# Gated linear attention with expert routing: the first expert search in a written order, all routing positions set anew, and a PSUM bank handed from the search results to the row transposes

## The chip, the cores and the metric

The kernel runs on one core of a Trainium2 chip. The metric is the device time of one execution in microseconds (us). The kernel before takes 435.39 us, the median of three runs (435.33 to 435.68). A difference of about 0.2% (0.9 us) is the least that such runs can tell from no change.

The engines are named as in the profile: PE is TensorE's matmul queue, PEld its weight loads, DVE is VectorE, ACT is ScalarE, POOL is GpSimd, SP is SyncE. Each of them works through its own instructions in order.

## The reference

The attention state is decayed by alpha and updated token by token. Its output is the input of a layer with eight experts, and routing goes by one sorted list of all (token, expert) logits:

```
for t in range(S):
    state = alpha[:, :, t, :, None] * state + einsum('bhd,bhe->bhde', k[:, :, t], v[:, :, t])
    y[:, :, t] = einsum('bhd,bhde->bhe', q[:, :, t], state)
x = y.transpose(0, 2, 1, 3).reshape(3072, 384)
logits = x @ w_gate                      # 3072 x 8
for idx in argsort(-logits.flatten()):
    tok, e = idx // 8, idx % 8
    if assigned[tok] < 0 and counts[e] < 384:
        assigned[tok] = e; counts[e] += 1
for e in range(8):
    mask = assigned == e
    out[mask] = maximum(x[mask] @ w1[e], 0) @ w2[e]     # 384 -> 1024 -> 384
```

Every expert ends with exactly 384 tokens, its capacity.

## The kernel before

**Routing in rounds.** The sorted list is not walked. A round takes for every token its best expert that is still open, finds the expert that fills up first and the logit at which it is full, and closes that expert. So there are eight rounds, one per expert, and the expert of a round is only known when its round is done. The key of a logit (a 32-bit integer) is cut into five digits (`BITS`, 7, 7, 6, 6, 6 bits). For each digit, one level of the search runs: DVE compares the digit with all its values (`compare`, the tile `cmp`), PE counts the tokens per expert at or above each value (24 matmuls into columns 32 to 39 of the tile `rt`, lines 581 and 614), DVE tests the counts against the places left (`g`), PE adds up the flags (`flags`, L599), DVE takes the largest (`k`, L601) and makes the next digit. After the last level the counts are kept (`cs`, L595), and `find` (L623) names the expert, starts its weight DMAs (`weights`, L528) and sums tokens per partition (`rts`). `offsets` (L655) is a matmul with a triangle of ones (`tri`), `places` numbers the tokens (`cum` ... `wb`, `bk`), `one_hot` (L694) builds the big table `hot` (128x3072) and `rhs`, `index` (L705) turns them into token numbers with 24 matmuls, and `gather` (L712) converts them on DVE (`idx`) and fetches the rows of x by three indirect DMAs on POOL's queue.

For the next round, `take_places` (L726) makes a one-hot column `oh` and closes the expert in the logits `L`; `gone` (L732) is one matmul that yields the tokens gone to each expert (columns 40 to 47 of `rt`); `best_left` (L737) is a chain of DVE operations from the maximum over `L` to the first digit `top`; `new_choice` (L759) makes `val`, `chu` and `o`; `left` (L774) subtracts what `gone` gave from `rem`.

**Where these results lie.** PSUM is used in banks of 128x512 FP32 values. One bank, `scr`, holds DVE's scratch columns (`slot`, L499). `rt` is a tile of its own in another bank, taken anew at every level. Further banks hold `h` (two), the three outputs `y0` to `y2`, and one bank, `xt`, in which rows and index results lie. Waits are set between instructions that touch the same PSUM bank, not only the same columns.

**The expert's work.** `split_hi` (ACT) and `split_lo` (POOL) cut the FP32 weights into a high and a low part, `whi` and `wlo`; `rows` (PE transposes, ACT copies) and `rows_lo` (DVE) do the same to the gathered rows (`xh`, `xl`). An expert has 144 products: eight units `ffn1` of nine matmuls (L835: three products of parts by three blocks of 128) and eight units `ffn2` of nine (L855). `ffn1`'s result goes through ACT (`hh`, L840) and DVE (`hl`, L841) to `ffn2`. A unit `ffn2` comes two `ffn1` units behind. From the third expert on, the first `ffn1` of an expert stands ahead of the last `ffn2` of the one before it.

**What sets the order.** All 1152 products stand in one list. Everything else that PE, DVE, ACT and POOL do during it is put in by position: `at(position, fn)` (L902) issues a routing step when that many products have been written. `levels` and `found` (L915, L919) place the five levels and the steps from `find` to `index` of the next expert; `renewed` (L926) places `take_places` and `gather` at an expert's base, `best_left` one product later and `gone` six products after the base. Of the engines' orders PE's is the one that carries the products, so a routing matmul whose input is late stops all products behind it.

**The start.** Attention ends at about 134 us. The first round's search can only then run its last four levels. Of the 96 transposes that bring the attention output back to rows (`y_trans`, L340, four to a group), 64 are left to be done between the search's steps. In this part the tile scheduler sets the order: `search(0)` (L563) ties each level's counts to a group of these transposes (`Y_IN_SEARCH`). Then follow, in written order, `find` to `gather` for expert 0, dummy matmuls (`spin_more`, L879), the first rows and the first level of the next round, and the products.

## Time and profile before

| quantity | before |
| --- | --- |
| median of 3 runs | 435.39 us (435.33 to 435.68) |
| the profiled execution | 433.69 us |
| its span | 431.8 us |
| mean granted TensorE clock | 0.969 |
| end of attention, first matmul of the first search's flags | 134.05 us |
| first product (ffn1 of expert 0) | 165.65 us |
| POOL busy | 279.9 us (65%) |
| ACT busy | 195.7 us (45%) |

The profile is of one execution. In the page, busy times are summed over instructions, and PE's ends are modelled: a matmul that overlaps the next is counted whole. In a timeline each row has the start, the busy time, the engine with line and operation, the output and the inputs, and in brackets how long the engine was idle before it and what released it. Rows of the same kind that follow each other are joined (x3), and their time is then that of the group. In a table of windows, each row is a stretch of the span with the busy time of each engine, and PEclk is the share of the full TensorE clock that was granted in it. The span lacks 1.9 us of the profiled execution's time, which lie before and behind it.

### The profile page before, as it was taken

What the parts mean: (1) busy time and instruction counts of PE and PEld (TensorE: products, weight loads), DVE (VectorE), ACT (ScalarE), POOL (GpSimd) and SP (SyncE); (2) the same over time, 40 slices, a digit from 0 to 9 for tenths busy, and PEclk for the clock granted to TensorE, in tenths of its full rate; (3) what the DMA queues carried; (4) which work ended last, traced back from release to release, by engine and by line L of the source; (5) the groups of instructions that cost most, each with busy time, mean ns of one, the idle gap of its engine ahead of it and who ended that gap; (6) DMA issues with size and microseconds to landing.
All of it is one profiled execution on the core that took longest, in us unless ns stands there. A gap on an engine that the chain in (4) does not pass through costs nothing.

```text
span 431.8 us, 10887 instructions
## 1 busy us (share of the span) xinstructions
PE 396.6 (92%) x4154; PEld 347.8 (81%) x4154; DVE 284.2 (66%) x838; ACT 195.7 (45%) x447; POOL 279.9 (65%) x327
## 2 busy tenths in 40 slices
PE   7999999989898858989999999999999997999993
PEld 3787777768676737989898899999999887999993
DVE  7888888878736497686697597687587576221210
ACT  1476666556565422424423534434434433644411
POOL 4668988677620026854687786776866865997802
PEclk9699999999999769999999999999999999999998
DMA  8999966660004584180180190191191198310101
GB/s 284 331 270 263 255 193 206 179 188 18 2 3 169 197 264 160 54 295 2 31 317 20 47 330 28 44 329 35 40 326 38 39 325 304 106 71 2 55 2 55
DMA packets 34467, 63.39 MB, mean 147 GB/s; under 512 B 3328, under 2 KB 14592, under 8 KB 34416
## 3 DMA queue, kind: packets, MB, share of 16 engines
q1 hardware_dynamic: 28176, 48.54, 36.0%
q0 software_dynamic: 3072, 9.44, 6.3%
q10 hardware_dynamic: 3168, 4.72, 3.1%
q8 instruction: 33, 0.54, 0.5%
q14 instruction: 18, 0.15, 0.1%
HBM read 53.25 MB, written 9.44 MB: 145 GB/s over the span
## 4 chain that ended last, share of the span: by engine, by line
PE 62%; DVE 21%; issue 6%; DMA 4%; POOL 3%; ACT 2%; SPq 0%; DVEq 0%; POOLq 0%; ACTq 0%
PE h L835 17%; PE y L855 16%; PE rt L614 6%; PE y L312 4%; PE y L306 4%; PE s L257 4%; DVE ga L226 3%; DVE sc L221 2%; DVE cmp L552 2%; PE xt L344 2%; DVE hot L699 2%; PE xt L249 2%; DMA raw_a<-in_alpha_dram 2%; PE xt L818 2%; PE xt L708 2%
## 5 line engine op out<-in xcount | busy, mean ns | idle before, releaser
L799 POOL TENSOR_TENSOR wlo<-w1r,whi 128x384 fp32r<-128x384 f32 x64 | 69.2, 1082 | 24.1 <-ACT whi L790 22.4
L799 POOL TENSOR_TENSOR wlo<-w2r,whi 128x384 fp32r<-128x384 f32 x64 | 68.0, 1063 | 25.6 <-PE xt L818 9.5
L840 ACT ACTIVATE hh<-h 128x384 fp32r<-128x384 f32 x64 | 31.5, 492 | 110.7 <-PE h L835 105.0
L841 DVE SCALAR_TENSOR_TENSOR hl<-h,hh 128x384 fp32r<-128x384 f32 x64 | 35.4, 553 | 51.8 <-ACT hh L840 50.6
L855 PE MATMUL y<-whi,hl 128*128 128x384 f32 x192 | 65.8, 343 | 0.0
L855 PE MATMUL y<-wlo,hh 128*128 128x384 f32 x192 | 65.8, 343 | 0.0
L855 PE MATMUL y<-whi,hh 128*128 128x384 f32 x192 | 64.9, 338 | 0.0
L716 POOL DMA_INDIRECT xr<-x_dram,idx x24 | 29.5, 1229 | 44.2 <-DVE asg L746 32.2
L269 POOL TENSOR_SCALAR_AFFINE_SELECT sm<-sm 128x512 f32<-128x512 f32 x48 | 29.4, 639 | 31.8 <-ACT sm L265 31.8
L835 PE MATMUL h<-xh,whi 128*128 128x384 f32 x192 | 47.5, 346 | 0.1
L835 PE MATMUL h<-xh,wlo 128*128 128x384 f32 x192 | 46.0, 344 | 0.0
L835 PE MATMUL h<-xl,whi 128*128 128x384 f32 x192 | 46.0, 344 | 0.0
L790 ACT ACTIVATE whi<-w1r 128x384 fp32r<-128x384 f32 x64 | 33.3, 520 | 25.0 <-PE y L855 10.8
L290 ACT ACTIVATE sb<-st,sc 128x48 f32<-128x48 f32 x80 | 24.6, 331 | 35.6 <-DVE st L297 21.2
L872 POOL DMA_INDIRECT out_dram<-yt,idx x24 | 25.0, 1043 | 18.4 <-ACT yt L859 14.6
L855 PEld LDWEIGHTS y<-whi,hl 128*128 128x128 f32 x192 | 36.2, 188 | 0.1
L855 PEld LDWEIGHTS y<-wlo,hh 128*128 128x128 f32 x192 | 36.2, 188 | 0.0
L855 PEld LDWEIGHTS y<-whi,hh 128*128 128x128 f32 x192 | 36.1, 188 | 0.0
L835 PEld LDWEIGHTS h<-xh,whi 128*128 128x128 f32 x192 | 33.6, 189 | 0.5 <-ACT xh L819 0.5
L835 PEld LDWEIGHTS h<-xh,wlo 128*128 128x128 f32 x192 | 33.8, 189 | 0.0
L552 DVE TENSOR_TENSOR cmp<-nd,iota 128x1536 bf16<-128x1536 bf16 (+4 forms) x32 | 33.1, 1044 | 1.0
L835 PEld LDWEIGHTS h<-xl,whi 128*128 128x128 f32 x192 | 33.6, 189 | 0.0
(177 smaller groups left out, 808.8 us busy)
## 6 DMA issues: line engine op xcount, KB each, us to landing
w1r<-in_moe_w_dram SPq DMA_DIRECT2D x16, 768.0 KB, 4.8
w2r<-in_moe_w_dram SPq DMA_DIRECT2D x16, 768.0 KB, 6.2
vt<-in_v_dram SPq DMA_DIRECT2D x24, 256.0 KB, 4.8
x_dram<-xg ACTq DMA_DIRECT2D x6, 768.0 KB, 3.7
raw_a<-in_alpha_dram SPq DMA_DIRECT2D x19, 226.2 KB
raw_k<-in_k_dram SPq DMA_DIRECT2D x19, 224.0 KB
raw_q<-in_q_dram SPq DMA_DIRECT2D x19, 224.0 KB, 5.2
raw_a<-in_alpha_dram SPq DMA_DIRECT2D x5, 258.5 KB, 5.0
```

The source lines that it names most:

```text
L269: nc.gpsimd.affine_select(SM[s][:, h], SM[s][:, h], pattern=[[0, 4], [1, C]], compare_op=OP.is_ge, fill=0.0, base=0, channel_multiplier=-1)
L290: nc.scalar.activation(SB[s, u][:, :D], St[p], AF.Copy, scale=ac)
L552: x = nc.vector.tensor_tensor(words(dst, nt, js), keyed(d, nt, js), each(iotas[t], nt, js), op=OP.is_ge)
L614: nc.tensor.matmul(rt[:, 32:40], st["cmp"][:, j // U, :, j % U], st["o"][:, j], start=(j == 0), stop=(j == NU - 1))
L716: g = nc.gpsimd.indirect_dma_start(out=XR[i][:, b], out_offset=None, in_=x_dram, in_offset=bass.IndirectOffsetOnAxis(ap=IDX[i][:, b:b + 1] ...
L790: nc.scalar.activation(hi[:, 0], a, AF.Copy)
L799: y = nc.gpsimd.tensor_sub(lo[:, h], x[h], hi[:, h])
L835: nc.tensor.matmul(o, a[:, 0, d], x[:, d], start=(n == 0), stop=(n == 3 * DB - 1))
L840: nc.scalar.activation(hh, o, AF.Relu)
L841: nc.vector.scalar_tensor_tensor(hl, o, 0.0, hh, op0=OP.max, op1=OP.subtract)
L855: nc.tensor.matmul(Y[b], a[:, bs], w[:, 1].rearrange("p a b -> p (a b)"), start=(q == 0 and n == 0), stop=(q == FB - 1 and n == 2))
L872: st_ = nc.gpsimd.indirect_dma_start(out=out, out_offset=bass.IndirectOffsetOnAxis(ap=IDX[i][:, b:b + 1], axis=0), in_=yts.pop((i, b)), in ...
```

## The change

Six things change.

1. The first round's search is no longer left to the scheduler. `search_first` writes its order: three transposes ahead of each flags matmul, 11, 8, 8 and 8 ahead of the counts of levels 1 to 4, and all that are left (14) behind the last flags. A group of four transposes may now be split. Its tables, and the first one-hot, are cut at two thirds instead of in halves. The tile `xg`, in which rows are collected on their way to DRAM, gets a third buffer.
2. `rt` is no longer a tile in a bank of its own. It is 64 columns of the bank `scr`.
3. The bank that this frees holds a second `xt`: the middle block of `rows` and, at the start, every other group of transposes go there.
4. All positions of routing steps change. From the third expert on, the levels stay near their places (35, 51, 67, 83, 99), `offsets` comes 15 products after `find` instead of 11, `one_hot` 28 instead of 24, and rows stand at 31, 38 and 45 after the base instead of 31, 48 and 60. For expert 1 the base moves from 76 to 98; for the last expert, `offsets`, `one_hot` and `index` stand 14, 14 and 18 products later.
5. The update of `L` moves from `take_places` into `best_left`, behind `idx`. The table of the next round's first level moves behind `new_choice` and `left`.
6. The first `ffn1` of an expert no longer stands ahead of the last `ffn2` of the one before; the second half of the weights' DMAs is issued behind the gather for every expert, not only for the first; there are fewer dummy matmuls; one `split_hi` less stands ahead of the first rows.

```diff
-TRI = 11
-HOT = 24
+Y_IN_LEVEL = (None, 11, 8, 8, 8)
+Y_BEFORE_FLAGS = 3
+SPIN = (16, 0, 2, 2, 2)
...
     ab_c, q0_c, bi_c = slot(NU), slot(NU), slot(NU, I32)
+    rt = slot(64)
...
         half(0)
-        if i:
-            half(1)
-        else:
-            second_half.append(half)
+        second_half.append(half)
...
-        return [slice(0, NU // 2), slice(NU // 2, NU)] if i == 0 else [slice(0, NU)]
+        return [slice(0, 2 * NU // 3), slice(2 * NU // 3, NU)] if i == 0 else [slice(0, NU)]
...
+    def search_first():
+        st["d"] = st["dig"][0]
+        st["g"] = g0
+        steps(Y_BEFORE_FLAGS)
+        nc.vector.tensor_copy(ramp_c, ramp)
+        nc.vector.tensor_copy(cst_c, cst)
+        flags(0)
+        for t in range(1, nb):
+            next_digit(t - 1)
+            parts = list(compare(0, st["d"], t, t == nb - 1))
+            steps(Y_IN_LEVEL[t])
+            for cmp, js in parts:
+                for j in range(js.start, js.stop):
+                    nc.tensor.matmul(rt[:, 32:40], cmp[:, j // U, :, j % U], st["o"][:, j],
+                                     start=(j == 0), stop=(j == NU - 1))
+            reached(t)
+            steps(Y_BEFORE_FLAGS)
             flags(t)
+        steps(4 * NS)
...
     def counts(t):
-        rt = st["rt"] = fps.tile([128, 64], F32, name="rt")
         for j in range(NU):
...
     def take_places(i):
         nt = st["nt"] + 1
         st["oh"] = rw.tile([128, 1], F32, name="oh")
         nc.vector.tensor_scalar(st["oh"][:nt], pcs[:nt], st["k"][:nt], None, op0=OP.is_equal)
-        nc.vector.scalar_tensor_tensor(L, col(cl_c), BIGNEG, L, op0=OP.mult, op1=OP.add)
 
     def gone():
         nt = st["nt"] + 1
-        nc.tensor.matmul(st["rt"][:, 40:48], st["oh"][:nt].to_broadcast([nt, 128]), st["cs"][:nt],
+        nc.tensor.matmul(rt[:, 40:48], st["oh"][:nt].to_broadcast([nt, 128]), st["cs"][:nt],
                          start=True, stop=True)
 
     def best_left(i):
         es, v = st["es"], st["v"]
+        nc.vector.scalar_tensor_tensor(L, col(cl_c), BIGNEG, L, op0=OP.mult, op1=OP.add)
         nc.vector.tensor_reduce(m_c, L, axis=X, op=OP.max)
...
-            o = psx.tile([128, DB, 128], F32, name="xt")
+            o = (fpt if b == 1 else psx).tile([128, DB, 128], F32, name="xt")
...
-            if i > 1:
-                units.insert(len(units) - 1, mine.pop(0))
             units += mine
...
-            offs = {0: 35, 1: 52, 2: 68, 3: 84, 4: 100} if loose else {0: 33, 1: 49, 2: 64, 3: 79, 4: 94}
-            end = 144 if loose else 133
-            renewed(base, i) if i < E - 1 else at(base, gather, i)
-            if i < E - 2:
-                at(base + 8, table, i + 1, 0)
-            if i < E - 1:
-                at(base + 9, new_choice, i)
-                at(base + 9, left, i)
-            at(base + 31, rows, i, 0)
-            at(base + (48 if loose else 45), rows, i, 1)
-            at(base + (60 if loose else 57), rows, i, 2)
+        offs = dict(enumerate((33, 49, 64, 79, 94) if i == 1 else (35, 51, 67, 83, 99)))
+        end = 137 if i == 1 else 144
+        renewed(base, i) if i < E - 1 else at(base, gather, i)
+        if i < E - 1:
+            at(base + 9, new_choice, i)
+        if i < E - 2:
+            at(base + 9, left, i)
+            at(base + 9, table, i + 1, 0)
+        for b, p in enumerate((31, 38, 45)):
+            at(base + p, rows, i, b)
```

`renewed` is not touched: `gone` still stands six products behind the base.

**First place: PE behind the index of an expert in the middle of the run.** Before, from the last of the 24 index matmuls:

```order
L708 MATMUL xt<-rhs,hot 128x3
L835 MATMUL h<-xh,whi 128x384 x3
L835 MATMUL h<-xh,wlo 128x384 [waits Pool_49]
L835 MATMUL h<-xh,wlo 128x384 x2
L734 MATMUL rt<-cs,oh 128x8 [waits DVE_49]
L835 MATMUL h<-xl,whi 128x384 x3
```

The same place now; L690 is the index, L816 the products, L715 `gone`:

```order
L690 MATMUL xt<-rhs,hot 128x3
L816 MATMUL h<-xh,whi 128x384 x2
L816 MATMUL h<-xh,wlo 128x384 [waits Pool_49]
L816 MATMUL h<-xh,wlo 128x384 x2
L816 MATMUL h<-xl,whi 128x384
L715 MATMUL scr<-cs,oh 128x8 [waits DVE_49]
L816 MATMUL h<-xl,whi 128x384 x2
```

`gone` stands six products behind the index in both. Its output is in `rt`'s bank before and in `scr`'s bank now; it waits for one DVE instruction in both. Before, this is `oh` (L729). Now it is the last operation of `best_left` that touches `scr`: `top` (L735) for experts 1 to 5, `val` (L730) for expert 6.

**The same place on DVE.** Before, from the update of `L`, which directly follows `oh`, to the first table of the next round:

```order
L730 SCALAR_TENSOR_TENSOR L<-scr,L 128x192
L713 TENSOR_SCALAR idx<-xt 128x3 [waits DMASW2_49,DMASW1_49,DMASW3_49,DMASW0_49,PE_49]
L739 TENSOR_REDUCE scr<-L 128x24 [waits DVE_49]
L740 SCALAR_TENSOR_TENSOR scr<-v,scr 128x24 [waits DVE_49]
L744 TENSOR_SCALAR sg<-scr 128x24 [waits DVE_49]
L746 SCALAR_TENSOR_TENSOR asg<-scr,es,asg 128x24
L747 TENSOR_TENSOR scr<-scr,sg 128x24 [waits DVE_49]
L748 TENSOR_TENSOR val<-L,scr 128x192 [waits DVE_49]
L749 TENSOR_TENSOR scr<-scr,shifts 128x120 [waits DVE_49]
L751 TENSOR_TENSOR scr<-scr,masks 128x120 [waits DVE_49]
L753 TENSOR_SCALAR top<-scr 128x24 [waits DVE_49]
L552 TENSOR_TENSOR cmp_98<-top,iota 128x3072 [waits DVE_49]
```

And now, from the update of `L`, which directly follows `idx` (L695), to the multiplication of `val` that belongs to `new_choice`:

```order
L720 SCALAR_TENSOR_TENSOR L<-scr,L 128x192
L721 TENSOR_REDUCE scr<-L 128x24 [waits DVE_49]
L722 SCALAR_TENSOR_TENSOR scr<-v,scr 128x24 [waits DVE_49]
L726 TENSOR_SCALAR sg<-scr 128x24 [waits DVE_49]
L728 SCALAR_TENSOR_TENSOR asg<-scr,es,asg 128x24
L729 TENSOR_TENSOR scr<-scr,sg 128x24 [waits DVE_49]
L730 TENSOR_TENSOR val<-L,scr 128x192 [waits DVE_49]
L731 TENSOR_TENSOR scr<-scr,shifts 128x120 [waits DVE_49]
L733 TENSOR_TENSOR scr<-scr,masks 128x120 [waits DVE_49]
L735 TENSOR_SCALAR top<-scr 128x24 [waits DVE_49]
L822 SCALAR_TENSOR_TENSOR hl<-h,hh 128x384 [waits Activation_49]
L743 TENSOR_TENSOR val<-val,scr 128x192 [waits PE_49]
```

The update of `L` has moved behind `idx`, and so into the chain that ends with `top`. The table (L552) has left this stretch. The multiplication of `val` now waits for PE, that is for `gone`, since both touch `scr`'s bank.

**Second place: DVE between `rts` and `rhs` of the same expert.** Before, its beginning and its end:

```order
L640 TENSOR_REDUCE rts<-scr 128x2 [waits DVE_49]
L841 SCALAR_TENSOR_TENSOR hl<-h,hh 128x384 [waits Activation_49]
L670 SCALAR_TENSOR_TENSOR cum<-ones_c,scr 128x24 x2
L672 TENSOR_SCALAR scr<-ramp,es 128x8 [waits DVE_49]
L674 COPY offs<-rt 128x2 [waits PE_49]
```

```order
L689 TENSOR_SCALAR wb<-scr 128x24 [waits DVE_49]
L691 TENSOR_TENSOR bk<-scr,bsel 128x72
L841 SCALAR_TENSOR_TENSOR hl<-h,hh 128x384 [waits Activation_49]
L699 TENSOR_TENSOR hot<-wb,iota 128x3072 [waits DVE_49]
L701 TENSOR_TENSOR rhs<-bk,scr 128x72 [waits DVE_49]
```

And now, the same two stretches:

```order
L625 TENSOR_REDUCE rts<-scr 128x2 [waits DVE_49]
L822 SCALAR_TENSOR_TENSOR hl<-h,hh 128x384 [waits Activation_49]
L653 SCALAR_TENSOR_TENSOR cum<-ones_c,scr 128x24 [waits PE_49]
L653 SCALAR_TENSOR_TENSOR cum<-ones_c,scr 128x24
L655 TENSOR_SCALAR scr<-ramp,es 128x8 [waits DVE_49]
L657 COPY offs<-scr 128x2 [waits DVE_49]
```

```order
L672 TENSOR_SCALAR wb<-scr 128x24 [waits DVE_49]
L674 TENSOR_TENSOR bk<-scr,bsel 128x72
L681 TENSOR_TENSOR hot<-wb,iota 128x3072 [waits DVE_49]
L683 TENSOR_TENSOR rhs<-bk,scr 128x72 [waits DVE_49]
L822 SCALAR_TENSOR_TENSOR hl<-h,hh 128x384 [waits Activation_49]
```

`cum` now waits for `offsets` on PE (the same bank again). The `hl` between `bk` and `hot` has moved behind `rhs`, and the one ahead of `cum` belongs to a later unit than before.

**Third place: PE between the flags of levels 2 and 3 in the first search.** Before:

```order
L599 MATMUL rt<-g,one_85 128x8 [waits DVE_49]
L344 MATMUL xt<-ident,yt 128x128
L344 MATMUL xt<-ident,yt 128x128 [waits Activation_49]
L344 MATMUL xt<-ident,yt 128x128 x3
L344 MATMUL xt<-ident,yt 128x128 [waits Activation_49]
L344 MATMUL xt<-ident,yt 128x128 x3
L344 MATMUL xt<-ident,yt 128x128 [waits Activation_49]
L344 MATMUL xt<-ident,yt 128x128 x3
L581 LDWEIGHTS cmp_99 [waits DVE_49]
```

And now:

```order
L585 MATMUL scr<-g,one_85 128x8 [waits DVE_49]
L343 MATMUL xt<-ident,yt 128x128 [waits Activation_49]
L343 MATMUL xt<-ident,yt 128x128 x3
L343 MATMUL xt<-ident,yt 128x128 [waits Activation_49]
L343 MATMUL xt<-ident,yt 128x128 x3
L568 LDWEIGHTS cmp_99 [waits DVE_49]
```

Thirteen transposes stood between the flags and the counts that follow; now there are eight.

More of the change, by code (lines that the diff above doesn't have):

```diff
@@ L611, in counts @@
     def counts(t):
-        rt = st["rt"] = fps.tile([128, 64], F32, name="rt")
         for j in range(NU):
@@ L722, in gather @@
                                   mybir.DependencyInfo(mybir.DependencyClass.Sync, mybir.DependencyReason.DATA),
-                                  reason="rows of the first expert before its later weights")
+                                  reason="an expert's rows before its later weights")
         second_half.clear()
@@ L865, in gla_moe_kernel @@
     scattered = []
-    apart = rw.tile([1, 1], F32, name="apart", bufs=1)
+    apart = rc.tile([1, 1], F32, name="apart")
     def scatter(i, b):
@@ new lines, in gla_moe_kernel @@
+    written = tc.manual_schedule(engines={E_.DVE, E_.PE, E_.Activation, E_.Pool})
+    written.__enter__()
+    search_first()
+    att.close()
+    rw = ctx.enter_context(tc.tile_pool(name="route_work", bufs=2))
+    wp = ctx.enter_context(tc.tile_pool(name="weights", bufs=2))
+    fp = ctx.enter_context(tc.tile_pool(name="ffn", bufs=2))
+    find(0)
+    offsets(0)
+    places(0)
+    one_hot(0)
+    index(0)
+    take_places(0)
+    gone()
+    spin_more(SPIN[0])
+    gather(0)
+    best_left(0)
@@ new lines, in gla_moe_kernel @@
+    left(0)
+    new_choice(0)
+    table(1, 0)
+    for q in range(3):
+        split_hi(0, q)
+    for n in range(3):
+        split_lo(0, n)
+    rows(0, 0)
+    counts(0)
+    rows_lo(0, 0)
+    reached(0)
+    spin_more(SPIN[2])
+    rows(0, 1)
+    rows_lo(0, 1)
+    spin_more(SPIN[3])
+    rows(0, 2)
+    flags(0)
+    rows_lo(0, 2)
+    next_digit(0)
+    table(1, 1)
+    split_hi(0, 3)
+    for n in (3, 4):
+        split_lo(0, n)
+    spin_more(SPIN[4])
+    levels(0, 1, {1: 15, 2: 28, 3: 41, 4: 55}, {})
```

270 lines of the change are left out of this document (99 added, 171 removed).

## The prediction

> **What bounds the kernel now.** I read the page first, then a table of windows, then PE's waits in the main stretch, and last the timelines of PE and DVE around the index of one expert.
>
> ```profile
> span 431.8 us, 10887 instructions
> PE 396.6 (92%) x4154; PEld 347.8 (81%) x4154; DVE 284.2 (66%) x838; ACT 195.7 (45%) x447; POOL 279.9 (65%) x327
> ```
>
> PE is the engine that hardly rests. The windows show where it does. The columns are the stretch, its length, the busy time of each engine with its instructions, the granted clock, the DMA share and the rate.
>
> ```profile
> 142.20:146.40 4.20, 4.20 (x42) 3.72 (x41) 1.61 (x5) 1.97 (x4) 0.00 (x0) 0.60 0.52 187
> 165.65:424.65 259.00, 249.97 (x2133) 235.06 (x2133) 159.09 (x471) 103.63 (x228) 181.64 (x192) 1.00 0.35 124
> 351.60:363.50 11.90, 8.85 (x73) 8.29 (x71) 9.05 (x30) 3.12 (x7) 6.76 (x8) 1.00 0.87 307
> ```
>
> From the first product to the last, 259.00 us, PE is busy for 249.97. Its own work cannot shrink, since the change neither adds nor removes a product. What is to be had there is 259.00 − 249.97 = 9.03 us. The waits of PE in that stretch account for nearly all of it:
>
> ```profile
> PE rt L663 <- DVE rts L653: 2.7, 1, 2.7
> PE rt L659 <- DVE rts L640: 2.1, 3, 1.1
> PE xt L708 <- DVE rhs L701: 1.5, 3, 0.7
> PE rt L614 <- DVE cmp L552: 1.3, 3, 0.7
> PE xt L818 <- DVE rem L775: 0.6, 1, 0.6
> PE xt L708 <- DVE xl L824: 0.3, 1, 0.3
> PE xt L818 <- DVE xl L824: 0.2, 1, 0.2
> PE xt L818 <- DVE chu L769: 0.2, 1, 0.2
> ```
>
> These are 8.9 us in 14 waits (three columns: total, times, longest). All end on DVE: routing results that PE reaches too early. Two things follow. Moving the positions can gain at most 9.0 us there. And any new wait of a PE instruction on a DVE chain is paid in full, since all products stand behind it.
>
> **Term C, the new wait of `gone`.** In the order of the changed kernel, `gone` waits for the last operation of `best_left` on `scr`, where it waited for `oh`. The trace has all it takes to price that. PE and then DVE, around the index of an expert in mid-run and around the last but one:
>
> ```profile
> 317.66 0.96 PE L708 MATMUL xt<-rhs,hot 128*128 128x3 f16 x24
> 319.63 0.29 PE L734 MATMUL rt<-cs,oh 65*128 65x8 f32 x2
> ```
>
> ```profile
> 318.66 0.16 DVE L713 TENSOR_SCALAR idx<-xt 128x3 int32<-128x3 f32 x1 [0.75 <-PE xt L708]
> 318.74 0.35 DVE L739 TENSOR_REDUCE scr<-L 128x24 f32<-128x192 f32 x1
> 319.12 0.19 DVE L740 SCALAR_TENSOR_TENSOR scr<-v,scr 128x24 f32<-128x24 f32 x1
> ...
> 320.98 0.18 DVE L753 TENSOR_SCALAR top<-scr 128x24 bf16<-128x24 int32 x1
> ...
> 351.67 0.16 DVE L713 TENSOR_SCALAR idx<-xt 128x3 int32<-128x3 f32 x1 [0.75 <-PE xt L708]
> ...
> 352.52 0.34 DVE L757 TENSOR_TENSOR val<-L,scr 128x192 bf16<-128x192 f32 x1
> ```
>
> PE reaches `gone` at 319.63, which is 0.97 after `idx` (318.66). `top` ends at 320.98 + 0.18 = 321.16. Now the update of `L` also stands between `idx` and that chain. An operation over the same 128x192 values takes 0.38 from start to start (318.74 to 319.12). The handing over to PE takes about 0.06, by these rows:
>
> ```profile
> 149.09 0.17 PE L599 MATMUL rt<-g,one 128*128 128x8 bf16 x1 [0.32 <-DVE cs L595]
> ```
>
> ```profile
> 148.88 0.15 DVE L595 COPY cs<-rt 65x8 f32<-65x8 f32 x1
> ```
>
> `cs` ends at 149.03 and the flags start at 149.09. So `gone` can start at 321.16 + 0.38 + 0.06 = 321.60, and PE stands 321.60 − 319.63 = 1.97 us. For experts 1 to 5 that is 5 × 1.97 = 9.85. For expert 6 the last operation on `scr` is `val`, which ends at 352.86; with 0.44 more this is 353.30, against PE's arrival at 351.67 + 0.97 = 352.64: 0.66. **C = +10.5** (9.5 to 11.2, by 0.2 us per expert in DVE's pitch). Expert 0's `gone` lies ahead of `best_left` and pays nothing. Nothing hides this wait: it is the products that are queued behind `gone`. On DVE the multiplication of `val` waits for `gone` in turn, and behind it stand `chu`, `o` and the first table, whose counts come 29 products later (29 × 0.1735 = 5 us).
>
> The row of 149.09 is also the evidence that the wait goes by the bank. That flags matmul writes columns 0 to 8 while `cs` reads 32 to 40 of the same tile, and it waits for `cs`. The Trainium skill, page "PSUM — Partial Sum Buffer", section "PSUM bank collisions raise a hardware error", states the rule in general: accesses of two engines are to be guarded by bank and 32-partition quadrant, not by address. Guarded by address, `gone` would wait for `oh` alone and the whole sum would end at −3.8 instead of +6.7; the trace agrees with the bank.
>
> **Term B, the waits that the new positions take away.** A product takes 0.1735 us (nine in a row, 407.29 back to 405.73, in a timeline quoted below, are 1.56). `offsets` comes 4 products later (0.7 us) in the rounds and 14 later (2.4 us, and 0.66 more by `gone`) for the last expert, `index` for expert 1 four products later behind `find`, its levels 13 to 14 products apart instead of 8 to 15. These shifts have the size of the waits listed. I take all of them as gone: **B = −9.0** (−9.0 to −8.0).
>
> **Term D, `index`, which now comes too early.** From `offsets` to `index` there are now 144 − 99 − 3 − 15 = 27 products and the rest of one, 28 in all, 28 × 0.1735 = 4.86 us. What must happen meanwhile: `cum` cannot start before `offsets` now, and ahead of it DVE does the `hl` of a unit that ends just before `offsets`.
>
> ```profile
> 406.77 0.68 PE L835 MATMUL h<-xl,whi 128*128 128x384 f32 x3
> 407.29 0.33 PE L855 MATMUL y<-whi,hh 128*128 128x384 f32 x1
> ```
>
> ```profile
> 405.73 0.68 PE L835 MATMUL h<-xh,whi 128*128 128x384 f32 x3
> ```
>
> ```profile
> 408.01 0.56 DVE L841 SCALAR_TENSOR_TENSOR hl<-h,hh 128x384 fp32r<-128x384 f32 x1 [2.56 <-ACT hh L840]
> ```
>
> ```profile
> 312.62 0.29 DVE L670 TENSOR_TENSOR_SCAN cum<-ones_c,scr 128x24 f32<-128x24 f32 x2
> 314.71 0.55 DVE L841 SCALAR_TENSOR_TENSOR hl<-h,hh 128x384 fp32r<-128x384 f32 x1
> 315.17 1.75 DVE L699 TENSOR_TENSOR hot<-wb,iota 128x3072 f16<-128x3072 bf16 x1
> 316.84 0.22 DVE L701 TENSOR_TENSOR rhs<-bk,scr 128x72 f16<-128x72 f16 x1
> ```
>
> From the end of a unit (407.29) to the end of its `hl` (408.57) it is 1.28. From `cum` to `hot` it is 315.17 − 312.62 = 2.55, of which an `hl` that now stands elsewhere takes 0.46 (314.71 to 315.17): 2.09. From `hot` to the end of `rhs` it is 317.06 − 315.17 = 1.89. The sum is 5.26 against 4.86: a wait of 0.4 per expert. There is a second cost. `hot` takes longer while POOL splits weights:
>
> ```profile
> 216.12 2.39 DVE L699 TENSOR_TENSOR hot<-wb,iota 128x3072 f16<-128x3072 bf16 x1
> ```
>
> ```profile
> 215.88 1.02 POOL L799 TENSOR_TENSOR wlo<-w1r,whi 128x384 fp32r<-128x384 f32 x1 [0.44 <-ACT whi L790]
> ```
>
> 2.39 with a split under way, 1.75 without: 0.64. The last two units of an expert's weights are split at about that time, and now need no longer wait for a buffer. I take 0.5, between 0 and the 0.95 or so of a whole split. **D = 6 × (0.4 + 0.5) = +5.4** (2.4 to 8.1).
>
> **Term A, the start.** Five transposes fewer stand ahead of the counts of levels 2 and 3, where DVE waits:
>
> ```profile
> 142.25 3.14 PE L344 MATMUL xt<-ident,yt 128*128 128x128 f32 x13
> 145.19 0.97 PE L581 MATMUL rt<-o,cmp 128*128 128x8 bf16 x24
> ```
>
> ```profile
> 142.94 1.03 DVE L552 TENSOR_TENSOR cmp<-nd,iota 128x768 bf16<-128x768 bf16 x2
> 146.20 0.17 DVE L582 TENSOR_TENSOR g<-rt,rem 128x8 bf16<-128x8 f32 x1 [2.23 <-PE rt L581]
> ```
>
> Thirteen take 145.19 − 142.25 = 2.94, eight 1.81, and the table is there at 143.97, before they end at 144.06: the counts start 1.1 earlier, for two levels 2.2. Against it: two constant copies now ahead of the flags, `cum` behind `offsets`, `L` behind `idx`, two more transposes in level 1, together some 1.0 (0.2 to 0.4 each, by rows like these). The 14 transposes left go under DVE's `find`. **A = −1.2** (−2.5 to +0.5, since the gather needs the last rows in DRAM, whose transposes come later).
>
> **Term E, small waits not seen before**: tables that meet a weight split as `hot` does, rows whose second bank is filled sooner, the last expert's `index`: **E = +1.0** (0 to 3).
>
> **At nothing.** The order of `ffn1` and `ffn2` at an expert's end: the last `ffn2` now follows two other units (18 products, 3.1 us), against 1.28 for `hh` and `hl`; uncovered it would cost 1.3 per expert. The second half of the weights lands behind the gather, about 14 us after `index` by the page's landings; the fifth split stands at product 80 (13.9 us) and its result is used over 4 us later. `xg`'s third buffer and the second row bank only lift waits of ACT and rows that B and A hold already.
>
> **The sum**: 10.5 − 9.0 + 5.4 − 1.2 + 1.0 = +6.7. The profiled execution took 433.69, with a span of 431.8; it lies 1.70 under the median of the runs, 435.39. So the span should be near 438.5, the profiled time near 440.4 and the median near 442.1.
>
> **Rivals.**
> 1. *Faster: the wait of `gone` costs nothing.* This decides if DVE is through with `best_left` within 0.97 us of `idx`, or if a matmul into other columns doesn't have to wait. Then C falls away: −3.8, 431.6 us. For it: the change is laid out as if six products were enough. Against it: 2.88 us of DVE work (0.38 and 321.16 − 318.66) and the row of 149.09. 7%.
> 2. *Gains and stall cancel.* C stays, but `hot` meets no split and chains are a little shorter than I add up: D and E at 0, A at −2.0: −0.5, 434.9 us. For it: D's two parts are small differences of long sums. 6%.
> 3. *The clock falls.* The pauses of 2 us in every expert could take PE to a lower clock. In 142.20:146.40 it was granted 0.60 over 4.20 us, a loss of 1.7; six such stretches on top of the forecast give 452 us. Against it: the kernel pauses for 2.7 us in 351.60:363.50 already (the wait for L653), at clock 1.00. The Trainium skill, page "TensorE: Matmul & The Clock Gate", section "What's actually happening", says that the clock is halved after an idle window of about 3.4 us. By that rule a pause of 2 us leaves the clock alone; the window row agrees. 5%.
>
> The forecast keeps 82%. Its own bounds, taken as independent (0.9, 1.0, 2.9, 1.5, 1.5), give about ±3.8, 438.3 to 445.9. To hold 8 in 10 with the second rival partly in it, I go to 436.5 below and 446.5 above. Faster by over 0.2% (0.9 us, about what a measurement can tell): the first rival, 0.07. Same: the second, 0.06. Slower: 0.87.
>
> **What would show it.** In the changed profile, PE's waits should have a row of `gone` (L715) for `top` (L735), five times with about 2 us each, and one of 0.7 for `val`. The rows of `rts` and `cmp` should be gone, and a row of `index` for `rhs` be there six times with 0.4 to 1. First product near 164.4. If `gone` has no such row, C is wrong and the kernel is faster; if `index` doesn't wait, D is, and the time is near 437.

## The result, and the profile after

The changed kernel takes 464.26 us, the median of four runs (461.51 to 465.31), against 435.36 for the kernel before. The ratio is 1.066 (95% interval 1.060 to 1.071): 29 us slower. The forecast was 442.1 with a range of 436.5 to 446.5. The sign was right, the size was not: the loss is four times as large.

The profiled execution took 463.28 us. The page of the changed kernel, its span and the granted clock in 40 slices:

```profile
span 461.6 us, 10860 instructions
PEclk9699999999999799899898978899997998999997
```

Before, the clock was at 9 in nearly every slice of the second half. Now it dips in many of them. Next is the table of windows over the products, from the first (163.55) to the last, and over two shorter stretches. The columns are length, PE's busy time with its instructions, clock, DMA share and rate:

```profile
163.55:454.55 291.00, 267.30 (x2133) 0.93 0.33 110
...
227.90:231.31 3.41, 3.41 (x13) 0.50 0.35 73
...
265.44:272.27 6.83, 5.75 (x19) 0.50 0.53 130
```

The stretch is 32.0 us longer than before (259.00). PE is idle for 23.7 us in it, 14.7 more than before. The other 17.3 us are busy time: the same 2133 instructions took 267.30 in place of 249.97, since PE ran at half clock in nine stretches of 3.41 or 6.83 us, like the two shown. The start is 2.1 us shorter, the end (7.1 us) is as before. 14.7 + 17.3 − 2.1 = 29.9, and the span grew by 29.8.

PE's waits in that stretch, with total, times and longest:

```profile
PE scr L715 <- DVE top L735: 10.3, 5, 3.0
PE scr L585 <- DVE g L604: 8.8, 4, 3.3
PE h L816 <- DVE hl L822: 2.5, 1, 2.5
PE xt L690 <- DVE rhs L683: 0.9, 5, 0.2
PE h L816 <- ACT xh L800: 0.6, 2, 0.4
PE scr L715 <- DVE val L739: 0.5, 1, 0.5
PE xt L690 <- DVE xl L805: 0.2, 1, 0.2
```

The two rows of L715 are the wait of `gone` that was forecast. The rows for `rts` and `cmp` are gone, as forecast. The second and third row, 11.3 us together, were not forecast. PE's timeline at one of each:

```profile
226.58 0.39 PE L715 MATMUL scr<-cs,oh 65*128 65x8 f32 x2 [1.83 <-DVE top L735]
...
245.46 0.17 PE L585 MATMUL scr<-g,one 128*128 128x8 bf16 x1 [1.83 <-DVE g L604]
```

DVE's timeline in the same two places:

```profile
223.64 0.16 DVE L695 TENSOR_SCALAR idx<-xt 128x3 int32<-128x3 f32 x1 [0.47 <-PE xt L690]
...
226.35 0.18 DVE L735 TENSOR_SCALAR top<-scr 128x24 bf16<-128x24 int32 x1
...
244.78 0.56 DVE L822 SCALAR_TENSOR_TENSOR hl<-h,hh 128x384 fp32r<-128x384 f32 x1 [3.48 <-ACT hh L821]
245.25 0.15 DVE L604 TENSOR_TENSOR g<-scr,rem 128x8 bf16<-128x8 f32 x1
```

At 226.58 `gone` starts 0.05 after the end of `top`. At 245.46 the flags wait for `g`, and `g` had its counts long before; it stood behind an `hl` that waited 3.48 us for ACT's `hh`. So the next view is ACT's timeline there, and POOL's:

```profile
243.87 0.49 ACT L840 ACTIVATE yt<-y 128x384 f32<-128x384 f32 x1 [4.15 <-DMA out_dram<-yt,idx]
244.26 0.49 ACT L821 ACTIVATE hh<-h 128x384 fp32r<-128x384 f32 x1
```

```profile
240.59 1.60 POOL L853 DMA_INDIRECT out_dram<-yt,idx  x1 [0.16 <-issue]
```

This is the whole chain at that place. ACT has to copy the last output block of an expert into `yt`. There are five such buffers, three per expert, so this copy needs the buffer that the scatter of the first block of the expert before gives back. That scatter is issued only at 240.59, after the expert's last product. ACT stands for 4.15 us, `hh` stands behind the copy, `hl` behind `hh`, `g` behind `hl`, the flags behind `g`, and all products behind the flags. ACT's waits in the stretch have it five times:

```profile
ACT yt L840 <- DMA out_dram<-yt,idx: 22.7, 5, 5.7
```

Before, there was no such row.

### The profile page after: what moved, and what is told of

It is laid out like the page before. It is cut to its first block, busy times and chain, and to the rows that moved or that the text cites. A ratio compares the mean times of both kernels' runs of the same rounds, so it can differ in the third digit from the quotient of the medians.

```text
span 461.6 us, 10860 instructions
## 1 busy us (share of the span) xinstructions
PE 413.0 (89%) x4150; PEld 361.3 (78%) x4150; DVE 285.0 (62%) x836; ACT 192.6 (42%) x447; POOL 270.5 (59%) x327
## 4 chain that ended last, share of the span: by engine, by line
PE 57%; DVE 19%; issue 7%; DMA 6%; POOL 5%; ACT 5%; SPq 0%; ACTq 0%; DVEq 0%; POOLq 0%
PE y L836 16%; PE h L816 15%; PE y L313 4%; PE scr L599 4%; DMA out_dram<-yt,idx 4%; PE y L307 4%; PE s L258 4%; POOL wlo L781 3%; DVE ga L227 2%; PE xt L250 2%; DVE sc L222 2%; DVE hot L681 2%; PE xt L799 2%; PE xt L690 1%; DVE hl L822 1%
## 5 line engine op out<-in xcount | busy, mean ns | idle before, releaser
L781 POOL TENSOR_TENSOR wlo<-w1r,whi 128x384 fp32r<-128x384 f32 x64 | 64.9, 1014 | 57.5 <-ACT whi L772 34.6
L781 POOL TENSOR_TENSOR wlo<-w2r,whi 128x384 fp32r<-128x384 f32 x64 | 65.0, 1015 | 23.3 <-DVE cmp L546 15.7
L836 PE MATMUL y<-whi,hh 128*128 128x384 f32 x192 | 69.2, 360 | 0.0
L836 PE MATMUL y<-whi,hl 128*128 128x384 f32 x192 | 69.0, 359 | 0.0
L836 PE MATMUL y<-wlo,hh 128*128 128x384 f32 x192 | 69.0, 359 | 0.0
L698 POOL DMA_INDIRECT xr<-x_dram,idx x24 | 23.1, 965 | 57.3 <-DVE L L720 48.2
L816 PE MATMUL h<-xh,whi 128*128 128x384 f32 x192 | 49.9, 364 | 3.1 <-DVE hl L822 2.5
L816 PE MATMUL h<-xl,whi 128*128 128x384 f32 x192 | 50.2, 361 | 0.0
L816 PE MATMUL h<-xh,wlo 128*128 128x384 f32 x192 | 48.3, 356 | 0.0
L816 PEld LDWEIGHTS h<-xl,whi 128*128 128x128 f32 x192 | 36.4, 203 | 9.1 <-issue 9.1
L816 PEld LDWEIGHTS h<-xh,whi 128*128 128x128 f32 x192 | 36.6, 204 | 4.1 <-DVE hl L822 2.8
L816 PEld LDWEIGHTS h<-xh,wlo 128*128 128x128 f32 x192 | 37.4, 203 | 0.0
L853 POOL DMA_INDIRECT out_dram<-yt,idx x24 | 29.1, 1212 | 13.4 <-ACT yt L840 9.5
L773 ACT ACTIVATE whi<-w2r 128x384 fp32r<-128x384 f32 x64 | 33.0, 515 | 2.6 <-DMA w2r<-in_moe_w_dram 2.6
```

The lines of the kernel that those rows point to most:

```text
L698: g = nc.gpsimd.indirect_dma_start(out=XR[i][:, b], out_offset=None, in_=x_dram, in_offset=bass.IndirectOffsetOnAxis(ap=IDX[i][:, b:b + 1] ...
L773: nc.scalar.activation(hi[:, 1], c, AF.Copy)
L781: y = nc.gpsimd.tensor_sub(lo[:, h], x[h], hi[:, h])
L816: nc.tensor.matmul(o, a[:, 0, d], x[:, d], start=(n == 0), stop=(n == 3 * DB - 1))
L836: nc.tensor.matmul(Y[b], a[:, bs], w[:, 1].rearrange("p a b -> p (a b)"), start=(q == 0 and n == 0), stop=(q == FB - 1 and n == 2))
L853: st_ = nc.gpsimd.indirect_dma_start(out=out, out_offset=bass.IndirectOffsetOnAxis(ap=IDX[i][:, b:b + 1], axis=0), in_=yts.pop((i, b)), in ...
```

## The experiments

**The two theories.** A: two waits make the loss, that of `gone` for its bank and that of ACT for an output buffer, and the falls of the clock follow from them. Its rivals, by run: the falls have a cause of their own, or the waits only move on. Four kernels were run first (runs 1 to 4), then four (5 to 8), then four (9 to 12), each group on another chip. The kernel before took 434.4, 434.3 and 436.0 us in the three groups. These medians lie further apart than the 0.9 us that were taken as the least difference ahead of the prediction, so across groups the ratios are to be compared, not the times.

**Run 1, `gone` ahead of `best_left`.**

```diff
         at(base, take_places, i)
+        at(base, gone)
         at(base, gather, i)
         at(base + 1, best_left, i)
-        at(base + 6, gone)
```

> The changed kernel with gone issued right behind take_places, ahead of best_left, so that it waits for oh and not for the end of best_left; the bank stays shared. Theory A (a pause costs its own length and then a fall of the granted clock, of 3.41 us or twice that): the six pauses of gone, 3.01 + 1.83 + 1.81 + 1.83 + 1.81 + 0.52 = 10.8 us, go, and with them the six falls of the clock that begin at them, 12.5 us of lost time: 464.3 - 23.3 = 441 us (438 to 444), with the pauses of flags for g and two to three falls of the clock still there. Rival 1 (the clock falls for another reason, such as the narrow index matmuls): 464.3 - 10.8 = 453.5, mean clock as low as 0.94. Rival 2 (the wait only moves on, to left or the counts of the first level): 460 or more.

446.94 us, ratio 1.027 (1.022 to 1.031). No wait of `gone` is left, and the time is 17 us less: outside the range of theory A, between it and rival 1. The profiled execution was the slowest of the five, 451.83. PE's waits in it show why the gain isn't 23:

```profile
PE scr L585 <- DVE g L604: 8.6, 4, 3.2
PE h L816 <- DVE hl L822: 5.2, 1, 5.2
PE scr L599 <- DVE cmp L546: 2.6, 5, 1.4
```

The wait for `hl` doubled, since PE now gets there sooner and the scatter doesn't, and the counts of the first level wait for their table, which the pause of `gone` had covered. The clock still fell six times in this execution, at these pauses.

**Run 2, six output buffers.**

```diff
-                        yt = yts[i, b] = fp.tile([128, Dm], F32, name="yt", bufs=5)
+                        yt = yts[i, b] = fp.tile([128, Dm], F32, name="yt", bufs=6)
```

> The changed kernel with six output buffers yt in place of five, so that the copy of an expert's last block no longer waits for the scatter of the expert before. Theory A: the pauses of flags for g (8.8 us in four) and of a product for hl (2.5) go, and the three falls of the clock at 244.9, 285.9 and 367.8 with them (6.8 us lost, less 1.3 that lies in the pauses): 464.3 - 11.3 - 5.5 = 447.5 (445 to 451); the six waits of gone stay. Rival (the copy is late because ACT or POOL is late, not for want of a buffer): no change, 462 to 466.

442.25 us, ratio 1.019 (1.011 to 1.027): 22 us less by one buffer. PE's waits for `g` and `hl` and ACT's for the scatter are gone; the six of `gone` are as they were:

```profile
PE scr L715 <- DVE top L735: 10.3, 5, 3.0
...
PE scr L715 <- DVE val L739: 0.5, 1, 0.5
```

The gain is 5 more than expected, because the clock fell only three times in the main stretch, not six: the same pause of 1.8 us sometimes brings it down and sometimes doesn't. It is also the forecast to the microsecond (442.1). That is partly chance: what the forecast put on `index` and on small waits (6.4 us) was 2, and the three falls of the clock (5.1 us) made up for it.

**Run 3, both.** The two edits together.

> Both edits: gone ahead of best_left and six output buffers. Theory A: all but the six waits of index go and the clock stays at 1.00 in the main stretch: 464.3 - 23.3 - 16.8 = 424 us (421 to 427), so faster than before by some 11 us; what the new positions and the first search bring, about 9 and 2, is then seen without cover. Rival (the two causes share their loss of clock, or a third wait comes up behind them): 430 or more.

427.42 us, ratio 0.982 (0.978 to 0.986): 7 us faster than before. In the table of windows PE's busy time is back at that of before:

```profile
164.19:419.00 254.81, 249.70 (x2133) 1.00 0.37 125
```

and these are all of its waits there:

```profile
PE scr L599 <- DVE cmp L546: 2.7, 5, 1.5
PE xt L799 <- DMA xr<-x_dram,idx: 1.0, 1, 1.0
PE xt L690 <- DVE rhs L683: 0.9, 5, 0.2
PE h L816 <- ACT xh L800: 0.6, 2, 0.4
```

Two edits of one line each take back all 29 us and 7 more. The cause of the loss is thereby shown. The expected 424 was 3 us too good, and its range was missed by 0.4, by the waits for `cmp` and for the last rows, which the pauses had covered.

**Run 4, six buffers, and dummy matmuls in `gone`'s pause.**

```diff
+    def keep_busy(n):
+        o = fpt.tile([128, DB, 128], F32, name="xt").rearrange("p a b -> p (a b)")
+        for _ in range(n):
+            nc.tensor.matmul(o, warm[:, :128], warm[:, :Dm], start=True, stop=True)
...
+        at(base + 6, keep_busy, {1: 18, E - 2: 3}.get(i, 11))
         at(base + 6, gone)
```

> Six output buffers, gone at its place with its wait, but ahead of gone PE does dummy matmuls into an idle bank (18 for expert 1, 11 for experts 2 to 5, 3 for expert 6), about as long as the pauses. To be read against the run with six buffers alone. Theory A, with the fall of the clock owed to PE's idleness: the time lost in the pauses stays (about 10.8 us, and up to 1 us more where the dummies last longer), the falls of the clock go: some 12 us less than the six-buffer kernel, 435 to 437. Rival (the clock falls because of something else than the pause): the same time as the six-buffer kernel or more.

436.25 us, ratio 1.0026 (1.0005 to 1.0047): 6 us less than run 2 by doing more work. The time is as expected; the gain is half of the 12 us expected, since run 2 had lost less by its clock. The timeline of PE at one of the pauses, and the window of all products:

```profile
225.02 1.96 PE L868 MATMUL xt<-warm 128*128 128x384 bf16 x11
226.99 0.39 PE L715 MATMUL scr<-cs,oh 65*128 65x8 f32 x2
...
165.49:428.75 263.26, 261.26 (x2199) 1.00 0.36 120
```

The 1.96 us are lost as before, but the clock did not fall once in the main stretch. The falls are thus owed to PE's idleness. Against run 3 the pauses alone, filled with dummies, cost 436.25 − 427.42 = 8.8 us.

**Run 11, half as many dummies.** The numbers are 9, 5 and 2 in place of 18, 11 and 3.

> As the six-buffer kernel with dummy matmuls ahead of gone, but half as many (9 for expert 1, 5 for experts 2 to 5, 2 for expert 6), so that about 1 us of each pause stays idle. Theory C (the clock falls when a stretch of 3.41 us holds too little work of PE, under about half): the falls are gone all the same, 436 us as with the full number, and less by up to 1 where the dummies there were too many. Rival (any idle pause of PE behind narrow matmuls brings the clock down): falls as in the six-buffer kernel, 440 to 442.

436.75 us, ratio 1.002 (0.999 to 1.005). PE's waits show that about half of each pause is idle again:

```profile
PE scr L715 <- DVE top L735: 5.5, 5, 1.5
...
PE scr L715 <- DVE val L739: 0.2, 1, 0.2
```

The clock did not fall in the main stretch. So it is not any pause that brings it down, but how much of one is in a stretch; the last section has the numbers.

**Run 5, the bank given back.** `rt` in a bank of its own, all row transposes in one bank, six buffers.

```diff
-    rt = slot(64)
+    rt = fps.tile([128, 64], F32, name="rt")
...
-    spare_bank[0] = fpt
+    spare_bank[0] = psx
...
-            o = (fpt if b == 1 else psx).tile([128, DB, 128], F32, name="xt")
+            o = psx.tile([128, DB, 128], F32, name="xt")
```

> The changed kernel with six output buffers and with rt back in a bank of its own; the second bank for row transposes is given up for it. gone stays six products behind the base. Theory A (the shared bank makes gone wait): no wait of gone for top, no fall of the clock in the main stretch, 427 to 430 us, so about what the kernel with gone moved ahead gave (427.4), plus up to 2 us in the first search, whose transposes have one bank less. Rival (gone pauses for its place in the order, whatever the bank): 440 to 443 as with six buffers alone. Rival 2 (the second transpose bank carries the gain of the new order): over 431, with waits of row transposes for their bank.

448.43 us, ratio 1.032 (1.026 to 1.037). Theory A's time was missed by 18 us, and the bound of rival 2 is met for a reason that it doesn't name. The edit took away more than the change had added: the kernel before also had two banks for the transposes in its first search. With one, PE waited 0.58 us for `xg` fourteen times, ran at half clock for 34 us, and the first product came at 178.22. In the main stretch `gone`, still six products behind the base, has no row among PE's waits, the largest of which in total is:

```profile
PE xt L799 <- DVE xl L805: 6.1, 7, 1.0
```

**Run 9, the bank given back behind the first search only**, with six buffers.

```diff
-            o = (fpt if b == 1 else psx).tile([128, DB, 128], F32, name="xt")
+            o = (fpt if b == 1 and i == 0 else psx).tile([128, DB, 128], F32, name="xt")
...
+    rt = fpt.tile([128, 4, C], F32, name="xt").rearrange("p u x -> p (u x)")[:, :64]
     levels(0, 1, {1: 15, 2: 28, 3: 41, 4: 55}, {})
```

> The changed kernel with six output buffers; rt lies in scr for the first round and from the first product on in the bank that the change gave to the middle rows, which go back to the one xt bank. gone stays six products behind the base. The earlier run with rt in its own bank throughout had no wait of gone, but lost 14 us at the start, where its transposes had one bank; this one keeps two there. Theory A: no wait of gone for top; rows wait for their one bank about 1 us per expert, as in that run; 427.4 + 4 = 431 us (429 to 434). Rival (gone's place is the cause, not the bank): 440 to 443.

436.23 us, ratio 1.002 (0.999 to 1.004): 2 more than the upper bound of theory A, 1.6 of which the kernel before was slower in this group too, and under the rival. `gone` does not wait at its place behind `best_left`. It was the bank. The clock fell once in the main stretch. PE waits for rows instead:

```profile
PE xt L799 <- DVE xl L805: 5.4, 6, 1.0
```

So the second row bank is worth having at these positions of the rows, and `gone` need only stand elsewhere.

**Run 6, the kernel before with `rt` in `scr`.**

```diff
+    rt_s = slot(64)
...
-        rt = st["rt"] = fps.tile([128, 64], F32, name="rt")
+        rt = st["rt"] = rt_s
```

(at all four places)

> The kernel before with one thing changed: rt is 64 columns of the scr bank. Theory A: gone waits for the end of best_left here too, 321.16 + 0.06 - 319.63 = 1.6 us for experts 1 to 5 and 0.3 for expert 6, 8.2 us in all; some of these pauses, with the narrow index matmuls beside them, bring the clock down for 3.41 us (1.7 us each, two to four of them): 434.4 + 8.2 + 3.4 to 6.8 = 446 to 449 us. Rival (sharing the bank alone costs little, it is the update of L in the chain or the new positions that make gone late): under 438.

447.23 us, ratio 1.029 (1.023 to 1.036), as expected. The new wait stands in the list of the kernel before:

```profile
PE scr L735 <- DVE top L754: 7.1, 5, 1.4
```

1.42 each, where 1.6 was worked out from the trace of before. In this execution 6.8 us were lost at half clock in the main stretch besides. The bank alone is enough; the new positions and the place of `L` only lengthen the wait.

**Run 7, the kernel before with the scatters 37 products later.**

```diff
-                for b, p in enumerate((56, 72, 88)):
+                for b, p in enumerate((93, 109, 125)):
                     at(base + p, scatter, i - 2, b)
```

> The kernel before with one thing changed: the scatters of an expert stand 37 products later (93, 109, 125 in place of 56, 72, 88), where the change put them against the products by moving the bases. Theory A: the copy of an expert's third output block finds no free buffer, ACT stands until a scatter has landed, and PE waits for g or hl behind it, four or five times 1.8 to 3.3 us, with a fall of the clock at some of them: 434.4 + 9 to 13 + 2 to 7 = 446 to 454 us. Rival (in the order of before, with the next expert's first ffn1 ahead of the last ffn2, the copy has room): under 438.

440.65 us, ratio 1.014 (1.007 to 1.021): slower, but between the theory and its rival. ACT waits for a scatter, though only twice, 2.7 us at expert 1 and 0.35 at expert 5:

```profile
ACT yt L859 <- DMA out_dram<-yt,idx: 3.1, 2, 2.7
```

The shift is not the whole of it. At expert 1 the 37 products put the scatter at 158 behind the expert's start, later than the 147 of the changed kernel. At experts 2 to 5 they put it at 147, as there, and ACT hardly waits. Two differences show in the traces. In the order of before, the next expert's first `ffn1` stands ahead of the last `ffn2`, so the copies come nine products (1.6 us) later against the scatters; the change took that away (its sixth part). And POOL issues the scatter of expert 1's first block when 141 products behind the start of expert 2 have begun, against 149 in the changed kernel, where the splits that stand ahead of the scatter have moved with it. How ACT's 22.7 us divide between shift, order and splits no run shows.

**Run 12, the scatters back.** The changed kernel with `gone` ahead of `best_left`, five buffers, and the scatters at 19, 35 and 51.

> The changed kernel with gone ahead of best_left, five output buffers as it has, and the scatters 37 products earlier (19, 35, 51 behind the base), where they stood against the products before the change. Theory A (the bases moved by 37 products and took the scatters with them past the end of an expert): no wait of ACT for a scatter, no pause of flags or of a product for hl, the same as with six buffers, 427.4 us (426 to 429). Rival (the buffers were too few for the new order of ffn1 and ffn2 in any case): 440 to 447.

436.88 us, ratio 1.003 (0.999 to 1.007), between run 1 (1.027) and run 3 (0.982), and between theory A and its rival. ACT's wait for a scatter is gone, so the shift had been its condition. But another pause of the flags appeared:

```profile
PE scr L585 <- DVE g L604: 4.8, 4, 1.2
```

It lies in the second level of four experts, where `g` starts 1.4 us after its counts have ended, while POOL issues two scatters. ACT's copy of the expert's last output block is late there too. What holds them the trace doesn't show; it stays open. The scatters' new place, between experts, is thus not bad in itself: with a sixth buffer (run 3) the kernel is faster than with the old place and five.

**Run 10, all positions and the order of units as before**, in the kernel of run 3 (the block of positions is that of the kernel before).

> The kernel with gone ahead of best_left and six output buffers, but with all positions of the kernel before and its order of ffn1 and ffn2; the first search in written order, the shared bank, the second row bank and the later weights stay. It splits the gain of 7 us: theory B (the positions take away 9 us of PE's waits and bring 5.2 of others): the main stretch goes back from 254.8 to 258 or 259, 431 us (430 to 433). Rival (the first search and the second bank bring it all): 427 to 428.

439.13 us, ratio 1.007 (1.004 to 1.010). PE's waits are those of the kernel before again, with a new one for the shared bank, the counts that wait until `left` has read `scr` (the last row):

```profile
PE scr L646 <- DVE rts L638: 2.7, 1, 2.7
PE scr L643 <- DVE rts L625: 2.4, 3, 1.2
PE scr L599 <- DVE cmp L546: 2.3, 2, 2.1
PE scr L599 <- DVE rem L758: 2.3, 5, 0.6
```

The positions are worth more than the 4 us expected: 11.4 us of waits against 5.2 in run 3. Another 6.8 us were lost at half clock in this execution, 5.1 of them in a stretch that begins at 168.1, right behind the first product. With the old positions the rest of the change gains nothing.

**Run 8, mended further**: the edits of run 3; the update of `L` back in `take_places`; the third round's levels at 40, 55, 68, 81 and 94, with the last two blocks of `rows_lo` at 48; the last expert's rows and `rows_lo` eight products later.

> The changed kernel mended: six output buffers, gone ahead of best_left, the update of L back in take_places, levels of the third round at 40, 55, 68, 81 and 94, and the last expert's rows eight products later. In the kernel with the first two edits PE still idles for 5.2 us in the main stretch, of which 1.45 and five times 0.3 are counts waiting for their first table and 1.0 is the last expert's rows. Theory: 0.38 of chain saved takes the 0.3 away, seven products the 1.45, eight the 1.0: 427.4 - 3.5 = 424 us (423 to 426). Rival (DVE is what sets the pace there and the waits move on): 427 or more.

426.59 us, ratio 0.980 (0.975 to 0.986). The waits for `cmp` and for the last rows went (2.6 us of waits are left in the main stretch, of 5.2), but one fall of the clock, at 202.5, took 1.7 us back. It is not clearly faster than run 3, and its range (423 to 426) was missed by 0.6. Both beat the kernel before by about 2%.

## Why the prediction was wrong, step by step

**C, the wait of `gone`: right.** 10.5 was forecast; it is 10.3 + 0.5 = 10.8. Experts 2 to 5 have 1.81 to 1.83 each (1.97 forecast), expert 6 has 0.52 (0.66). Expert 1 has 3.01, because there an `hl` that waits for ACT stands between `idx` and the update of `L`. That the total is so close is partly luck: expert 1 is 1.0 over and the five others are 0.7 under together.

**B, the waits that go: right.** Of the 14 waits of before three are left, all at an index and shorter: 0.17 and 0.20 at experts 2 and 3, 0.22 at the last. They are counted under D.

**D, `index`: five times too large.** Five waits for `rhs` of 0.16 to 0.20 and one of 0.22 for `xl`, 1.1 us in all in place of 5.4. The chain is 0.2 us shorter than its pieces added up to. And for experts 1 to 6 no `hot` met a split: at 220.70 it took 1.75, not 2.39. Only the last expert's did, at 397.36, with 2.08. The collision had been put into the sum without a look at when the splits would run. Its row was also misread: the `hot` of 1.75 at 315.17 did have a split beside it. That split began at 315.40, and it was the split that took longer, 2.40 in place of 1.0. What made `hot` long at 216.12 was a split already under way when it began.

**A, the start: not shown.** The first product came 2.1 us earlier in this execution. But over the ten kernels with the same start, one execution each, it came from 163.55 to 166.41, at 165.2 in the mean. The kernel before had it at 165.65, run 7 with the same start at 163.93, and run 6, whose first search has `rt` in `scr`, at 166.48. The written order of the first search gains nothing that these runs can tell.

**E and what was put at nothing: the first step that failed.** The prediction weighed the order of `ffn1` and `ffn2` at an expert's end by the wait of `ffn2` for `hh` and `hl` alone. It did not follow the other thing that an expert's end starts, the copies into `yt`, to what gives `yt` back. And it followed each moved step but one: the bases went from 54 (65 at expert 1) to 91 products behind an expert's start, with everything that is placed from a base. The positions of the scatters, 56, 72 and 88, are not in the diff as changed lines. They moved all the same, from 110 (121 at expert 1) to 147 products behind that start, past the expert's end at 144. This made 11.3 us of PE's waits, and in run 2 one more buffer took 22 us with the clock.

**Rival 3, the clock: right, with 5% on it, and the second step that failed.** The forecast put falls of the clock at nothing; they cost 17.3 us of busy time in this execution. The rival was argued away by one pause of 2.7 us at full clock, and by the page "TensorE: Matmul & The Clock Gate" of the Trainium skill, section "What's actually happening", by which an idle window of about 3.4 us halves it. The length of 3.4 us is right: each fall lasts one or two such windows. That the window must be idle is not: pauses of 0.5 to 3.3 us were enough here, though not each time. The measurement decides. The row on which the argument rested was near the edge, as the last section shows. Rival 3 would have given 452, and with the scatters' waits of 11 us on top about the measured time. That is luck in part: the clock took 17 us and not 10, at pauses of both kinds, and D and E took some 4 less than forecast.

The page "PSUM — Partial Sum Buffer" of the Trainium skill states in "PSUM bank collisions raise a hardware error" that accesses are to be guarded by bank and not by address. The waits of this program are set like that: run 6 has the wait of `gone` with the shared bank, run 9 has none without it. In all these kernels, and in the row of 149.09 on which the prediction relied, the shared bank is also one tile, so no run here tells a guard by bank from one by tile, and none shows what would happen without the wait.

## What to carry to other kernels

When a base moves, list everything that is placed from it, and above all what the diff doesn't show: transfers that give buffers back. Follow a buffer once round, from the copy that needs it to the transfer that frees it, and see which of them comes first now. A pause of PE cost more than its length here once it left a clock window less than about half full. Dummy work in the pause kept the clock, and half as much did too (runs 4 and 11).

## What the runs showed of the hardware

In these traces the clock changes in windows of 3.41 us on a fixed grid. All falls of one execution start a whole number of 3.41 us apart: in the changed kernel at 190.36, 227.90 (11 windows on) and 265.45 (11 more). From the 14 profiles of this case I took every window of this grid that lies wholly between the first and the last product and ran at full clock. In each I took PE's busy time less that of the narrow matmuls, that is of counts and index (24 with 8 or 3 columns each, 0.96 us together). Products, dummies and row transposes are left, which I call wide.

| busy time less counts and index | windows | with half clock in the next |
| --- | --- | --- |
| under 1.50 us of 3.41 | 22 | 22 |
| 1.50 to 1.79 us | 20 | 7 |
| 1.80 us and more | 996 | 0 |

The bounds were chosen after the fact, and the ends of matmuls are modelled. With the time of the wide matmuls added up by itself, where they overlap narrow ones too, two falls lie above 1.80, at 1.90 and 2.07 us. So the edge is known only roughly, between 1.5 and 2.1 us.

The narrow matmuls keep PE busy, but by these windows they do not keep the clock. The window from 384.92 of the changed kernel held 2.72 us of busy time in all, 0.96 of it narrow, and the clock fell behind it. The one from 401.98 held 1.91 us, all of it wide, and the clock stayed. No run changed the narrow matmuls alone. In the changed kernel, two windows at the edge; behind the first the clock fell, behind the second it didn't:

```profile
224.49:227.90 3.41, 1.58 (x10) 1.00 0.44 115
326.89:330.30 3.41, 1.61 (x10) 1.00 0.00 0
```

And this is the pause of the kernel before on which the prediction relied, in its own window:

```profile
353.76:357.17 3.41, 1.71 (x10) 1.00 0.94 314
```

1.71 us of products: in the middle class, where the clock fell behind about one window in three. It was luck, not a margin. What decides in that class the traces don't show.
